# A new order for the 1284 listed jobs of a sketched-attention and mixture-of-experts kernel

## The chip, the core and the metric

The kernel runs on one core of one Trainium2 chip. The metric is the device time of one execution in microseconds. The engines are called by the profile's names: PE (matrix products; PEld loads their weights), DVE (VectorE), ACT (ScalarE), POOL (GpSimd) and SP, which here does nothing but issue DMAs. Each engine runs its instructions in the order in which the program lists them.

## The reference, cut to what matters

For 4 batches of 1088 rows, a polynomial attention is computed from sketches of q and k, and its output x (1088 by 128 per batch) goes into an attention with 4 experts, of which 2 are chosen per row.

```python
phi(x) = outer(S1 @ x, S2 @ x)                 # 8 x 8 = 64 features per head and row
kv, z  = phi(k).T @ v, phi(k).sum(rows)
x      = (phi(q) @ kv) / (phi(q) . z + 1e-6)   # 4 heads of 32 side by side: 128 columns
logits = x @ w_gate                            # the 2 largest of 4 experts, softmax weights w
a_e    = softmax(causal(scale * (x wq_e)(x wk_e).T))
out    = sum over the 2 chosen e of w_e * (a_e @ (x wv_e) @ wo_e)
```

## The kernel before

The kernel is a list of 1284 small jobs. Each `job(...)` has a name, one engine or a choice of two, its estimated length, what it reads and makes, and which buffers it holds. `Plan.run` (line 85) walks the text `ORDER` (line 21), a list of job numbers, and emits the jobs in that order. A letter behind a number says which of the two engines takes the job: for a copy `a` is ACT and `b` is DVE; for a product of features it depends on the job; for an idle matmul pair (`dummy`) `a` is PE and `b` leaves it out. A buffer from a pool goes to the next holder in the order of the list, so the list also decides who waits for which buffer. No engine reorders anything; a job that waits holds up all later jobs of its engine.

The work of one batch b has these stages, and the stages of neighbouring batches overlap.

- **Loads** of k, q and v (SP, for batch 0 also ACT). Batch 0's q comes in four loads, q0.0 and q0.2 on SP, q0.1 and q0.3 on ACT (line 436); k in two (line 430).
- **Batch 0's head** (`prepare`, `attend_rows`). DVE transposes k and q (`turn k0`, line 484; `turn q0`, line 494). PE projects them with the sketch (`project k0`, `k0+`, `q0`, `q0+`, line 562; the + parts hold the later columns). ACT or DVE copies half of each result (`low`), DVE adds the other half (`lift`, line 574), and DVE or POOL multiplies out the 64 features (`multiply`, line 580): two products for each of k0 and k0+, one for q0 and three for q0+. PE sums k features with v (`sums 0`, line 619), turns the q features (`turn qf`, line 666), multiplies by the sums (`numer 0`, line 692); DVE divides, PE turns x back.
- **Batches 1 to 3** (`prepare`, `attend_turned`): `sketch k`, `sketch q` (line 523), `back` (line 527), `features` (line 537), `sums` (line 627), `keep sums`, `repeat sums`, `fifth`, `keep rep`, `keep fifth`, `turn f` (line 805), `numer` (line 827), `turn rows` (line 839), stores of x and fetches of it in rows (line 857).
- **Choice of experts** (`choose_experts`): logits, comparisons, masks of bf16 that are stored to and fetched from memory (`fetch masks`, line 999; batch 0's first third is widened on PE instead, `widen`), `exponents`, `shares` (lines 945 to 957, POOL), `scale`.
- **Attention**: the 17 tiles of 64 rows of a batch come in groups 0 to 2 of 6, 6 and 5. `query b.n` (line 1066), `base`, `pick` (line 1079, needs the masks), `score b.i` (line 1104), `take` (line 1116, DVE), `exp` (ACT), `guard` (ACT or POOL), `invert`, `weigh` (line 1147, POOL), `turn A` (line 1152, DVE), then `sum b.n.j` (line 1180, PE, needs every `turn A` of its group), `keep V`, `patch V`, `spread V` (line 1207, POOL), `out` (lines 1251, 1277, 1301), `turn out`, `keep out`, `store out`.

PE has four pairs of PSUM banks for all of this. Group 0 of batch 3 is the last; its four expert products (`out 3.0.x`) end the kernel's matmuls, then three pieces are copied (`keep out 3.0.0` to `.2`) and stored.

Two small chains matter besides. The constant tables: `decode` (DVE) unpacks S1 and S2, `spread1` to `spread3` and `diagonal0` to `diagonal3` copy the tables into place on DVE, POOL and ACT, `rep16`, `repeat S2` (PE, line 362) and `keep S2` repeat one of them. And the gate: `load w4` fetches w_gate, `gate order` (POOL, line 294) reorders it, and all logits need it.

`dummy0` to `dummy39` are pairs of bf16 matmuls of 512 columns on a zeroed tile (line 250); their results are not used.

Of the kernel before, what the change touches and what calls it, by code (L numbers as in the profile page):

```python
# [24 lines left out]
61 414 403 130 134 419a 154 72 407 131 135 155 138 417a 75 73 408 412 136 74 23b 132 404 160 77 188 133a 161 137a 187  # L25
156 76 158 416a 162 163 166 157 141 192a 159 167a 164 190 191a 170 177 189 175 418a 165a 420 176 692 171 693 139 421
172 178 193 65 194 422b 411 423 140 209 210 195 182 196 66a 691 183 694 230 424 211 197 425 216 179 173 701 184 174a
428a 427a 143 180 202 231 181 702 426a 203 198a 232 199 212b 200 204 429 168 233a 153 217 254 253 185 201 213 205a 206
234 207 145 214 142 218 431 10b 430 208 258a 235 144 219a 257a 236 438 223 432 215 255 256 698 224 220 326 259 697 439
221 440 169a 327 329 225 260 148 330a 331a 226b 328 261 146 227 433 228 299 300 149 332 275 276 222 262 333 442a 283  # L30
301 441a 186a 284 229 263 277 268 434 264a 700 278 237 285 269 435a 238 436a 279a 270 437 271a 302 265 147 705 239 443
280 708 266 286 706 287a 281 272 282 240a 444 6b 32b 709a 243a 241a 303b 244 358 712a 273 304 245 305 274 151 359 446a
707a 445a 242a 267 711a 291 292 306 350 288 367 360 289 699 351 361 362a 366 293 294 369 290 343 246 26b 295a 368 713a
696 370 342 363 296 710a 344 14b 33b 345 297 247 464 465 371 364 298 447 715 714 352 466 695 467 469 703 307 372a 353
15b 354a 716a 717 346b 308 309 310 355 468 373 450 993 21b 474 718 721a 475 311 470 312 722a 719 316a 365 374 375 704
471 451 334 313b 347 335 314a 25b 720a 479 480 318 317 356 482 315b 336 723 481 348 320 484a 483a 448 357 43b 485 319
22b 337 321 323 338b 339 340 725 486 515 322 724 732 349 501 986 994 324a 516 517 547 548 341 494 449 487 502 503 495
488 733 508 476 509 472 726 990 510 546 734 545 727 376 377 477 736b 496 987 378 550a 150 379 489 992 549a 497a 380
504a 728 490b 511b 988 27b 518b 730a 498 519 152 735a 505 551 729b 522 381 478b 506 985 499 491 552 507 382 383 737
384 560 453 523 989 456 461 731 31b 385a 500 457 386b 592 512 513 492 389 591 520 39b 561 387b 388a 738 454 593 40b  # L40
41b 248 390 514 249 575 576 996 250 392 524 740b 525a 594 391 493 739a 526 251a 995 577 521 460 578 562 325 452 567
527 568 553 569 595a 563b 570 528 455 554 999 596 579a 7b 458 1002 580 473 555 758 619 13b 618 38b 759 1000 623a 529
760 571a 761 762 572 581 622b 624 530 556a 564 531 565 557 533a 620 597 532a 558 582 621 462 573 566 537 393 535a 534a
536 625 538 539 394 583 1001a 584 763 559 585 651 598 998 463 459 768 395 642 650 652 19b 20b 1004a 634 643 635 773
1005a 574 636 658 659 774 644 397 764 653 586 661 775 1003a 645 777a 660 776 1007b 1006a 646b 647 587a 778a 765 662
779 588 589 991 654b 627 648 769 663 780 637 664b 626 1009 590 1008 638b 599 600 628 649 655 1010b 1012 665 601 997
629 666 639 640 1011 602 603 741 1016a 630b 252 604 1015a 656 667 657 398 631 641 607a 606a 1013 770 541 605b 610 744
540 742 609 542 788 608b 789 816 543a 809 1014b 743 632 633 817 612 790 810 1017 1018 668 1019 811 1020 1021 745 669
781 795 818 670 671 672 782 783 796 812a 819b 1026 611 1027 791a 792 771 673 1028 1029a 674 772a 784b 793 797 785 675
1030a 676 1031 1022 677b 678b 681 842 1024a 679a 682 813 748 840 839 396 1023a 844a 841 802 747 680a 786 814 1025 803  # L50
804 615 614 843b 766 683 798b 613 820 794 845 815 805a 846 799 616b 1032 821 806 847 878 848 787 807 877 684 869 1034a
1033a 753 749 800 870 822 854 879 801 871 1052 913 808 912 862 855 861 849 856 885 1053 1054 886 914 746 767 1055 1056
872 916a 863 873a 850b 917a 751 851 918 852 915 874 617 823 864 824 887 825 875 888 919 865a 685 755 857a 750 853 921
37b 889a 866 880 42b 827a 826a 24b 858 1057 867 829a 868 876 1058 828b 544 920 890 831 830 859 686 860 689 922 923
881b 945 944 955 946 891 953 952 954 936 832 882 892 937 833 938 1139 754 947 30b 948b 924b 1138 44b 1141 1143a 956
1062 929 1140 883 1063 1060 884 1142a 925 836 957 1144 926 928 752 939 958a 1145 959 927 756 834 835 940a 1169 930
1168 941 931 1064 688 1170 837b 932a 1185 1184 960 961 838 1065 933 942 893 894 1186 949 950 943 895 951 896 934 1171
897 898 902a 935 901b 962 963 964 900b 1035 899a 1039 903 965 757 1172a 1146 1036 966 967 1187 1037 968 904 1147 969
970 1177 971a 1038 1153 972b 975 1176 906 974a 1042 976 905 973b 1212 1154 1043 1178 1155 1188a 1156a 1160 16b 17b
1179 978 1180a 1213 1061 1161 1211 1173 690 1214 907 908 1049 1157 909 1216a 1050 1148 1066a 1044 1189 9b 977 1190  # L60
1162 1059 1215a 1158 1191 1163 1164a 1217 1068 1067 1181 1149b 1174 1182 1218 1251 1071a 1252 687 1041 910a 1048 1040
1175 1183 1227 1254 1165 1150 1159 1228 1253 1255 1256 1046 1045 1166 1072b 1229 1244 1257b 1243 1230 1151 1245 1152
1073 1051 34b 1070 1069 1219 1167 1258 1220 1221 979 1074 1236 1231b 1232 1047 980 1259 1235 29b 1075 1246 1222 1247a
1223a 1192 1248 1237 1193 1224 1233 1249 1076 1234 1250 1194 1238 1110 1096 1239b 1260 1195 1225 36b 1226 1240 1097
1111 1089 1103 1241 1112 1242 1090 983 1196 1104 1197 1098 1099b 982 1105 1091 1261 1262 981 1113b 1198b 1201b 1199b
1114 1200a 1106b 1202 1263 1082 1264 1100 1265 1083 1204 1266 1077 1084 1107 1085b 35b 1101 1203 1267 984 1092b 1102
1115 1268 1205 1078b 1079 1108 1116 1086 1269 1093 1208 1087 1273b 1207 1094 1270b 1088 1274 1080 1095 8b 1272a 1206
# [1323 lines left out]
```

## Time and profile before

| | us |
|---|---|
| median of 3 runs (265.70 to 266.31) | 265.95 |
| profiled execution, its own time | 265.45 |
| its span, first to last instruction | 263.7 |
| PE busy | 256.1 (97%) |
| DVE busy | 208.5 (79%) |
| POOL busy | 161.0 (61%) |
| ACT busy | 104.3 (40%) |

The time of an execution holds the span and 1.75 us around it. Rows of the profile name an instruction by its line, engine and operation, and by the buffers that it writes and reads (`out<-in`), with shapes; `x` is a count. A bracket behind a row of the timeline is the idle time of the engine ahead of it and what ended it. Matmuls in 32-bit floats are two records each, and they are pipelined, so that records overlap. In tables by stretches the columns are busy time and count of PE, PEld, DVE, ACT and POOL, the granted clock, the share of DMA and GB/s.

### The profile page before, as it was taken

To read this page: it belongs to the slowest core of one execution; us is meant where nothing else is said; L and a number is where in the kernel's file an instruction comes from. 1 tells how busy PE (TensorE), PEld (TensorE's weight loads), DVE (VectorE), ACT (ScalarE), POOL (GpSimd) and SP (SyncE) were. 2 spreads that over 40 slices of the span, in tenths; PEclk is the share of its full clock that TensorE was granted. 3 is DMA by queue.
4 is the path that set the end of the run, shared out by engine and by line. 5 is a ranking of instruction groups with operands and counts; after the bars stand their busy time and mean duration, and the time that the engine had idled before them with its cause. 6 is when DMAs were issued, how large, how long until landed. Compare 5 with 4: busy or idle time off the path is not lost.

```text
span 263.7 us, 9228 instructions
## 1 busy us (share of the span) xinstructions
PE 256.1 (97%) x3807; PEld 193.4 (73%) x3807; DVE 208.5 (79%) x531; ACT 104.3 (40%) x278; POOL 161.0 (61%) x265
## 2 busy tenths in 40 slices
PE   7979999999999999999999999999999999999994
PEld 2967666755968877665797975665798875689984
DVE  5597999989998798999987288988885469895451
ACT  2333564665542315524613134635503164333020
POOL 6498478699677725198494894274734282533841
PEclk9999999999999999999999999999999999999999
DMA  7985769960288859806050390626114599210012
GB/s 149 187 144 144 145 144 177 175 134 1 46 169 162 124 149 213 149 14 149 2 88 4 83 167 30 163 51 152 14 32 81 103 221 194 50 44 2 5 32 56
DMA packets 87740, 27.35 MB, mean 104 GB/s; under 512 B 58577, under 2 KB 87057, under 8 KB 87697
## 3 DMA queue, kind: packets, MB, share of 16 engines
q1 hardware_dynamic: 85040, 26.08, 51.8%
q10 hardware_dynamic: 2656, 0.67, 1.1%
q8 instruction: 30, 0.49, 0.8%
q14 instruction: 14, 0.11, 0.2%
HBM read 22.22 MB, written 4.52 MB: 101 GB/s over the span
## 4 chain that ended last, share of the span: by engine, by line
PE 85%; DVE 9%; DMA 3%; issue 1%; ACT 0%; SPq 0%; ACTq 0%; DVEq 0%
PE pair L1180 28%; PE pair L1104 23%; PE pair L1066 10%; PE pair L1301 6%; PE pair L1251 3%; DMA mb<-md 3%; PE pair L523 3%; PE pair L627 3%; PE pair L827 2%; DVE fp L580 2%; PE pair L562 2%; DVE qs L1079 1%; DVE w L1116 1%; PE pair L1277 1%; DVE fp L805 1%
## 5 line engine op out<-in xcount | busy, mean ns | idle before, releaser
L1147 POOL TENSOR_SCALAR w<-w,rs,sh 128x448 f32<-128x448 f32 (+16 forms) x68 | 55.5, 822 | 39.8 <-DVE rs L1143 38.1
L1104 PE MATMUL pair<-xT,qs 128*128 128x384 f32 (+11 forms) x216 | 73.6, 477 | 0.3 <-DVE qs L1079 0.3
L1132 ACT ACTIVATE w<-w,mx 128x384 f32<-128x384 f32 (+16 forms) x68 | 52.4, 772 | 53.3 <-DVE mx L1116 45.9
L1116 DVE CUSTOM_DVE_ANT_0 w<-pair,mask 128x576 f32<-128x576 f32 (+13 forms) x68 | 48.5, 726 | 13.1 <-PE pair L1104 12.4
L1104 PEld LDWEIGHTS pair<-xT,qs 128*128 128x128 f32 x216 | 38.4, 190 | 24.9 <-issue 11.9
L1152 DVE STREAM_TRANSPOSE AT<-w 128x64 f32<-128x64 f32 (+16 forms) x68 | 50.8, 761 | 6.9 <-POOL w L1147 6.7
L1180 PE MATMUL pair<-AT,xra 32*128 32x160 f32 (+5 forms) x1136 | 44.9, 303 | 0.0
L1180 PEld LDWEIGHTS pair<-AT,xra 32*128 32x128 f32 x1136 | 41.7, 185 | 4.2 <-DVE mx L1116 1.8
L1207 POOL TENSOR_TENSOR agg<-agg,mb 128x768 f32<-128x768 f32 (+1 forms) x22 | 34.0, 1559 | 14.8 <-PE pair L1180 5.8
L1066 PE MATMUL pair<-xT,Mq 128*128 128x384 f32 (+1 forms) x96 | 33.7, 476 | 0.0
L193 ACT COPY agg<-pair 128x384 f32<-128x384 f32 (+1 forms) x27 | 11.8, 470 | 49.2 <-PE pair L1180 33.8
L1180 PEld LDWEIGHTS pair<-AT,xrb 32*128 32x128 f32 x752 | 26.3, 185 | 2.1 <-issue 2.0
L1180 PE MATMUL pair<-AT,xrb 32*128 32x160 f32 (+5 forms) x752 | 27.7, 289 | 0.0
L537 POOL TENSOR_TENSOR fp<-w 128x576 f32<-128x576 f32 x21 | 24.9, 1201 | 1.6 <-DVE w L527 1.1
L1066 PEld LDWEIGHTS pair<-xT,Mq 128*128 128x128 f32 x96 | 17.4, 190 | 10.9 <-issue 2.4
L1079 DVE COPY_PREDICATED qs<-mb,pair 128x768 f32<-128x768 uint16 (+1 forms) x24 | 23.1, 963 | 0.7 <-DMA mb<-md 0.3
L1301 PEld LDWEIGHTS pair<-Mo,agg 128*128 128x128 f32 x168 | 20.0, 192 | 2.2 <-issue 0.7
L1301 PE MATMUL pair<-Mo,agg 128*128 128x128 f32 x168 | 20.8, 277 | 0.0
L193 DVE COPY agg<-pair 128x384 f32<-128x384 f32 (+1 forms) x19 | 9.5, 519 | 9.7 <-PE pair L1180 9.7
L1140 POOL TENSOR_SCALAR rs<-zs 128x1 f32<-128x1 f32 x31 | 6.6, 213 | 17.1 <-ACT w L1132 12.9
L1143 DVE RECIPROCAL rs<-rs 128x1 f32<-128x1 f32 x68 | 9.1, 144 | 8.0 <-POOL rs L1140 6.6
L193 ACT COPY qs<-pair 128x384 f32<-128x384 f32 (+1 forms) x21 | 9.3, 455 | 10.9 <-PE pair L1066 10.9
(179 smaller groups left out, 311.7 us busy)
## 6 DMA issues: line engine op xcount, KB each, us to landing
xra<-xd SPq DMA_DIRECT2D x16, 192.0 KB, 5.5
xrb<-xd SPq DMA_DIRECT2D x16, 192.0 KB, 5.6
xrc<-xd SPq DMA_DIRECT2D x16, 160.0 KB, 5.1
mb<-md SPq DMA_DIRECT2D x4, 576.0 KB, 7.1
mb<-md SPq DMA_DIRECT2D x4, 480.0 KB, 6.9
mb<-md SPq DMA_DIRECT2D x6, 288.0 KB, 4.9
in<-in_k_dram SPq DMA_DIRECT2D x12, 136.0 KB, 3.1
in<-in_q_dram SPq DMA_DIRECT2D x3, 544.0 KB, 4.7
```

What stands on the lines that cost most here:

```text
L193: (nc.scalar.copy if eng == "ACT" else VEC[eng].tensor_copy)(o, i)
L537: VEC[e].tensor_tensor(out=f, in0=a[:, :, None, R : 2 * R].to_broadcast([128, j1 - j0, R, R]), in1=a[:, :, 0:R, None].to_broadcast([128, j ...
L1066: nc.tensor.matmul(plan[ps[x]][:, y, 0:w], Mq[:, ((1, 2), (0, 3))[x][y]], plan[xT][:, 64 * t0 : 64 * t1], start=True, stop=True)
L1079: nc.vector.copy_predicated(chosen(), rows(c), rows(plan[ps[x]]))
L1104: nc.tensor.matmul(plan[p][:, y, 0 : c1 - c0], plan[qs][:, 128 * t : 128 * t + 128], plan[xT][:, c0:c1], start=True, stop=True)
L1116: nc.vector.tensor_tensor_reduce(out=o, in0=src, in1=msk, scale=-1.0, scalar=mx[:, b, i, x - 1 : x] if x else 3e38, op0=ALU.add, op1=ALU.m ...
L1132: nc.scalar.activation(out=a, in_=a, func=ACTF.Exp, bias=mx[:, b, i, last : last + 1], scale=-1.0, accum_out=zs[:, b, i : i + 1])
L1147: nc.gpsimd.tensor_scalar(out=a, in0=a, scalar1=rs[:, b, i : i + 1], scalar2=plan[("sh", b)][:, i : i + 1], op0=ALU.mult, op1=ALU.mult)
L1152: nc.vector.transpose(dst[:, 0 : keys // 32, t], plan[A][:, 0:keys].rearrange("p (j s) -> p j s", s=32))
L1180: nc.tensor.matmul(plan[Vk[g // 2]][:, g % 2, lo : 32 * nt], plan[(f"xr{j // 12}", b)][rows, j % 12], a[rows, j, lo:], start=(j == 0), sto ...
L1207: nc.gpsimd.tensor_tensor(out=a, in0=a, in1=plan[mb][:, 2 * x : 2 * x + 2, 0:w], op=ALU.mult)
L1301: nc.tensor.matmul(plan[p][0:m, 0, 128 * x : 128 * x + 128], plan[agg][:, e, 128 * x : 128 * x + m], Mo[:, e], start=(e == 0), stop=(e == ...
```

## The change

Only the text `ORDER` differs: the same 1284 jobs in another order, with 87 of the choices of engine turned over. Line numbers stay as they are.

```diff
 ORDER = """
-0 1 2 3 4 78 79 46 12a 28a 5a 64 45 82 80 62 48 18a 55b 85 84 86 81 83 87 53b 56 11a 52b 54b 90 91 94 95a 96 98b 99 58
-92 93 104 100a 105a 88a 89b 101 108 68 97a 109a 400 399 103a 114 402 401 50 102b 49 110 106 115 113b 117a 57 59 107a
-111b 116b 124 51 125a 63 112a 406 118 70 120 60 409 410 119a 122 69 121a 47 126 123a 413 127 405 128 71a 415 67 129a
...
-1271a 1109 1276 1081 1117 1118 1119 1209a 1275 911 1277 1278 1210 1124a 1120b 1121 1122 1126 1125 1123a 1279 1128
-1127a 1281 1280 1129 1130 1282 1131 1136a 1137b 1283 1134b 1132a 1133b 1135a
+0 1 2 3 4 78 79 83 15a 80 45 21a 48 46 10a 81 90 53b 52b 91 54b 50 25b 18a 49 55b 5b 12a 14a 51 82 84 87 85 86 94 64
+63 95b 96 27a 57 56 58 92 99 93 98b 100a 65 104 97a 101 400 89b 66a 108 103a 88a 105a 114 68 69 106 102b 70 109a 401
+115 71a 110 116a 117a 107a 113a 402 399 118 124 111a 112a 59 60 120 61 406 119a 410 125a 122 405 121a 126 67 403 409
...
+1270a 1202 1115 1116 1081 1100 1205 1206 1101 1207 1208 1102 1274 1085b 1273a 1086 1275 1272b 1209a 1087 1088 1117
+1277 1118 17b 43b 6b 1276 1119 982 1124a 1120b 1121 1122 1210 1123a 1278 1126 1279 1128 40b 1129 23b 1125 29b 1281
+1283 1282 1127a 1130 1131 1280 1132b 1134b 37b 1133a 1136a 1135a 1137b
```

The head of the two lists, engine by engine:

```text
PE   before: 5 idle pairs | project k0 | project k0+ | project q0 | project q0+ | turn w0 | sums 0.0 | sums 0.1 | turn qf 0.3 | turn qf 0.0 | turn w2 | turn qf 0.1 | turn qf 0.2 | turn w1 | numer 0.0 | sketch k1
PE   after:  6 idle pairs | project k0 | 1 idle pair | project k0+ | repeat S2 | project q0 | project q0+ | sums 0.0 | turn w0 | turn w1 | turn w2 | sums 0.1 | turn qf 0.0 | turn qf 0.3 | turn qf 0.1 | turn qf 0.2 | numer 0.0 | sketch k1
DVE  before: decode | turn k0 | lift k0 | turn q0 | lift k0+ | multiply k0.0 | multiply k0+.1 | lift q0+ | lift q0 | multiply q0.0 | keep sums 0.0 | spread3 | multiply q0+.1 | turn k1
DVE  after:  decode | turn k0 | spread3 | low k0 | lift k0 | turn q0 | multiply k0.0 | lift k0+ | multiply k0+.1 | lift q0 | lift q0+ | multiply q0.0 | multiply q0+.2 | multiply q0+.0 | multiply q0+.1 | turn k1
POOL before: const | pick8 | ident | rep4 | diagonals | multiply k0.1 | spread v1 | multiply k0+.0 | spread1 | multiply q0+.2 | multiply q0+.0 | rep16 | mask | onehot | gate order | features k1
POOL after:  ident | const | diagonal2 | spread1 | diagonal3 | pick8 | rep16 | multiply k0.1 | spread v1 | multiply k0+.0 | gate order | onehot | rep4 | features k1
ACT  before: load q0.1 | load q0.3 | diagonals | low k0 | low k0+ | low q0 | spread v0 | low q0+ | spread2 | keep sums 0.1 | keep qf 0.3 ...
ACT  after:  load q0.3 | load q0.1 | diagonals | spread2 | low k0+ | keep S2 | spread v0 | low q0 | low q0+ | keep w | keep sums 0.0 | keep sums 0.1 | keep qf 0.0 ...
SP   before: load q0.2 | load q0.0 | loads of v | w0 | w2 | loads of k1 | w1 | w3 | v1.2 | w4
SP   after:  load q0.0 | load q0.2 | loads of v | w1 | w0 | w2 | loads of k1 | w3 | w4
```

Further on, the runs of `score`, `sum`, `query`, `sketch`, `numer` and `out` follow each other on PE in the same large order, with other neighbours inside the runs. `repeat S2` (65) stood on PE between `sums 1.1` and the first scores. `turn rows 3` (1035) now precedes the last `turn A` of batch 2, and `shares 3.0` (1064) comes right ahead of `weigh 2.13` (934) on POOL. `fetch masks 3.2` (1061) no longer follows two fetches of x on SP, and `spread V 2.1.1` (906), whose buffer it takes over, comes behind `scale 3.0` (1066) and `weigh 3.9` (1174) on POOL. At the end `turn out 3.2` (1279) precedes `mix V 3.0.1` (1125) on DVE, `keep out 3.0.0` goes from ACT to DVE, and its store from ACT to SP.

Of the 87 turned choices, 8 are idle pairs (7 are run where 5 were), 29 are `guard` (15 from ACT to POOL, 14 back), 37 are `keep` copies (17 from ACT to DVE, 20 back), and the rest single copies, products, one `scale` and one store.

More of the change, by code (lines that the diff above doesn't have):

```diff
@@ L27 @@
[L27 to L46, printed above, removed]
@@ new lines @@
+1147 1066a 1174 906 1148 1149b 1156a 907 1150 1212 1211 1157 971a 909 1175 972a 1189 974a 976 1037 1158 1061 1151 975
+1038 1160 1216b 1161 973b 1214 1215a 1190 978 1046 1217 1213 1051 1191 1040 1176 1177 1218 1178 1152 1044 1162 977
+1179 908 1049 1228 1159 1227 1180a 1219 1220 1251 1163 1181 1059 910a 1182 1229 1164b 1254 1165 1252 1042 1221 1253
+911 1166 1230 1068 1067 1072a 1244 1070 1231a 1071a 1069 690 1183 1255 1243 1167 1236 1232 1073 1256 1074 1235 1257a
+1222 1245 1075 979 1223b 1224 1258 1041 1233 1237 36b 1246 1225 1043 1047 980 1259 1234 1076 1260 1192 1247a 1238 1048
```

60 lines of the change are left out of this document (37 added, 23 removed).

## The prediction

> **What bounds the kernel now.** I read the busy shares first, then the chain that ended last, then busy time by stretches.
>
> ```profile
> PE 256.1 (97%) x3807; PEld 193.4 (73%) x3807; DVE 208.5 (79%) x531; ACT 104.3 (40%) x278; POOL 161.0 (61%) x265
> PE 85%; DVE 9%; DMA 3%; issue 1%; ACT 0%; SPq 0%; ACTq 0%; DVEq 0%
> ...
> 36.00:56.00 20.00, 19.75 (x297) 12.81 (x296) 19.44 (x53) 11.67 (x38) 15.28 (x28) 1.00 1.08 170
> 76.00:208.00 132.00, 132.00 (x2066) 100.59 (x2064) 107.04 (x259) 49.17 (x132) 78.34 (x121) 1.00 0.49 96
> 208.00:220.00 12.00, 11.75 (x58) 8.21 (x57) 9.30 (x23) 6.20 (x18) 7.96 (x12) 1.00 1.03 198
> ```
>
> The fourth row's first busy figure is PE: 132.00 of 132.00. The two other stretches lose 0.25 us each. So from some 20 us on PE sets the end, and a new order of the same matmuls can win only where PE waits or does useless work: in the head and in the tail. In 36 to 56 DVE is as full (19.44 of 20.00), which matters below.
>
> The head, by the order of time on PE:
>
> ```profile
> 1.31 4.45 PE L250 MATMUL pair<-idle 128*128 128x512 bf16 x10 [1.31 <-DVE idle L243]
> 6.33 6.33 PE L562 MATMUL pair<-SD,in 128*128 128x128 f32 x36 [0.57 <-DVE in L484]
> ...
> 20.66 1.60 PE L523 MATMUL pair<-in,SK 32*32 32x288 f32 x64
> ...
> 6.30:8.40 2.10, 2.07 (x10) 2.10 (x11) 1.00 1.24 253
> 8.40:10.50 2.10, 2.10 (x11) 2.10 (x11) 1.00 1.25 200
> 10.50:12.50 2.00, 2.00 (x19) 1.97 (x17) 1.00 0.76 120
> ```
>
> Ten idle matmuls, a hole of 0.57 us, then the projections (L562); the last three rows are those alone. They come 10 or 11 in 2.1 us before 10.5 and 19 in 2.0 us after it: PE runs at half pace up to there. From L523 (sketch k1, 20.66) on, PE is full. I measure the head by when sketch k1 can start. What holds it is a chain on DVE:
>
> ```profile
> 4.78 1.41 DVE L484 STREAM_TRANSPOSE in<-in 128x576 f32<-128x576 f32 x2
> 8.82 0.42 DVE L574 TENSOR_TENSOR w<-pair,w 128x256 f32<-128x256 f32 x1 [2.64 <-ACT w L193]
> 9.16 1.36 DVE L494 STREAM_TRANSPOSE in<-in 128x384 f32<-128x384 f32 x2
> 11.01 0.49 DVE L574 TENSOR_TENSOR w<-pair,w 128x320 f32<-128x320 f32 x1 [0.48 <-ACT w L193]
> 11.41 3.12 DVE L580 TENSOR_TENSOR fp<-w 128x512 f32<-128x512 f32 x2
> 14.46 0.81 DVE L574 TENSOR_TENSOR w<-pair,w 128x384 f32<-128x384 f32 x2
> 15.30 1.73 DVE L580 TENSOR_TENSOR fp<-w 128x768 f32<-128x768 f32 x1
> ...
> 17.19 0.81 DVE L193 COPY SK<-SK 32x48 f32<-32x48 f32 x1
> 18.03 0.85 DVE L580 TENSOR_TENSOR fp<-w 128x512 f32<-128x512 f32 x1
> 18.81 1.36 DVE L488 STREAM_TRANSPOSE in<-in 128x512 f32<-128x512 f32 x2
> ```
>
> DVE waits 2.64 us for project k0 and its copy, 0.48 for project k0+, and is then busy until the last feature (18.88) and turn k1 (20.17), which lets sketch k1 go.
>
> **The change, part by part. Idle matmuls.** Six pairs now run ahead of project k0, one more than before: 12 at 0.43 (4.45 for 10) from 1.31 end near 6.5, against a start at 6.33. The extra pair is hidden to 0.2 us by turn k0, which runs to 6.19. The seventh, ahead of project k0+, costs 0.43 to 0.86 there; its cover is turn q0 and multiply k0.0 on DVE, which now come before lift k0+; without that cover the whole chain is late by as much. What the filled hole does to the pace no row shows. Bounds: fast from the start of project k0, or from 10.5 as now. Project k0 (8 records) then takes 0.85 to 1.7 us and ends between 7.4 and 8.3; I take 7.8, in the middle, and keep both.
>
> The Trainium skill ("TensorE: Matmul & The Clock Gate", Part 1) says that the array's rate doubles after a busy window of about 3.4 us, and that the windows run free of the kernel's start. By it a filled hole brings the rise one window forward or changes nothing, as the phase falls; the doubling in the rows agrees.
>
> **Features on VectorE.** Low k0 moves from ACT to DVE (an ACT copy in either place: about 0.4), spread3 (0.81 of the chain now, at 17.19) goes into DVE's idle time before it, two multiplies of q0 move from POOL to DVE. Prices:
>
> ```profile
> 15.15 2.81 POOL L580 TENSOR_TENSOR fp<-w 128x512 f32<-128x512 f32 x2 [0.53 <-DVE w L574]
> ...
> L537 DVE TENSOR_TENSOR fp<-w x3: 695/753/793, 87.1 to 124.9; 128x576 f32<-128x576 f32 x3
> ...
> 11.57 1.17 ACT L193 COPY vp<-w 64x1152 f32<-64x1152 f32 x1
> 12.70 0.48 ACT L193 COPY w<-pair 128x384 f32<-128x384 f32 x1
> 2.10 1.07 ACTq L436 DMA_DIRECT2D in<-in_q_dram  x2
> ...
> in<-in_q_dram ACTq DMA_DIRECT2D x2, 136.0 KB, 5.2
> ...
> 10.54 2.57 SPq L436 DMA_DIRECT2D in<-in_k_dram  x4
> wgr<-in_moe_w_gate_dram SPq DMA_DIRECT2D x1, 2.0 KB, 3.1
> ```
>
> The same product costs DVE 0.695 for 576 elements in its cheapest record (1.21 ns each) and 1.73 for 768 (2.25 ns) while POOL multiplies beside it from 15.15. The four q multiplies are 2304 elements: 2.8 us without POOL, 5.2 beside it. In the new list POOL's next job after its two k products is the copy of w_gate (gate order), and that load is issued behind the four loads of k1. These begin when project k0+ is done and take 2.57 to issue; the load of w_gate takes 3.1 to land. With project k0+ done near 9.5, that is past 15; POOL then stands still for much of the q features. I take 3.2.
>
> DVE, worked forward: low k0 from 7.9 (0.4), lift k0 0.42, turn q0 1.36: to 10.1. The q loads are shared out in another order over the same two queues, all four are needed, and the last of ACT's row lands 5.2 after an issue near 2.6, so by 7.8: cost nothing, and 0.9 us of cover (turn q0 begins at 8.7). On SP the load of w1 goes ahead of the k1 loads; the queue stands still before 10.54 anyway. Multiply k0.0 (512) 0.6 to 1.15, say 0.8, to 10.9; lift k0+ 0.49; multiply k0+.1 1.8 (768 elements, POOL beside it) to 13.2. Low q0 and low q0+ on ACT follow the copy of v, which stays at 11.57 if v lands as now: 1.17, about 0.3 (low q0 has half the columns of the 0.48 row) and 0.48, to 13.5, so the second lift ends near 14.0. Features 3.2 to 17.2, against 18.88: 1.7 earlier. Turn k1 follows to 18.6 (the k1 loads, issued a little earlier, have landed by then), and PE reaches sketch k1 over its last turn of q features and numer 0.0 by the same 1.7 earlier. The ends: features 2.8 and a fast pace, 2.5 gained; features 5.2 and a slow pace, 0.8 lost.
>
> The skill ("SBUF — State Buffer", Who interferes with whom) says that a VectorE instruction with two SBUF inputs and a GpSimd one that reads SBUF lock each other out for a whole instruction. 1.73 against 0.93 for 768 agrees. By it POOL's later casts, if w_gate lands early, hold up one feature each; then the sum is 266.4, as the second rival has it.
>
> **The stretch after sketch k1.** Repeat S2 moves from here into the head, where PE waits anyway:
>
> ```profile
> 33.29 0.63 PE L362 MATMUL pair<-ident,rep 32*128 32x32 f32 x4
> 33.85 1.46 PE L1104 MATMUL pair<-xT,qs 128*128 128x192 f32 x6
> ```
>
> Start to start it held PE for 0.56: gained. Counting runs of one kind of matmul after sketch k1, the new list has 73 where the old has 70. A change of kind has no row of its own; between nothing and 0.28 each (half of the 0.56, which holds two changes and the work), I take 0.13: 0.4 lost. The macro order of PE (which score, sum, sketch and query runs follow each other) is the same, so its load is. DVE takes the small copies keep rep 1.0 and keep fifth 1 and gives keep sums 1; none has more columns than the copy of 0.29 in the tail's rows, so up to 0.3 is lost in the full stretch, and I count 0.3. The 87 jobs that change engine are mostly guards (15 one way, 14 back) and V copies (17 against 20): level.
>
> The one wait there that the chain shows:
>
> ```profile
> 208.78 6.91 DMA mb<-md
> ```
>
> The masks of batch 3 landed at 215.7 and cost PE 0.25 of 208 to 220. In the new list their fetch no longer stands behind two fetches of x on SP, but spread V 2.1.1, which frees its buffer, stands behind two more jobs on POOL: level. Waits of a new list at new places can't be read here; the old one has 0.5 us in two stretches. I allow 0.5 more, with 0 and 3 as ends.
>
> **The tail.**
>
> ```profile
> 259.80 0.29 DVE L193 COPY ob<-pair 128x128 f32<-128x128 f32 x1 [1.94 <-PE pair L1277]
> 260.78 0.27 ACT L193 COPY ob<-pair 128x128 f32<-128x128 f32 x1 [0.45 <-ACT ob L193]
> 261.07 0.37 ACTq L1283 DMA_DIRECT2D out_dram<-ob  x1
> ```
>
> The last store waits on ACT behind another copy and store. Its copy moves to DVE (259.80 and 260.1) and its store to SP, so the last issue starts near 260.5: 0.5 gained. Turn out 3.2 goes ahead of mix V 3.0.1 on DVE, which out 3.0.1 needs two matmul groups later: 0 to 0.1.
>
> **Sum** on the profiled execution (span 263.7, time 265.45): -1.7 - 0.56 + 0.4 + 0.3 + 0.5 - 0.5 = -1.56, or 263.9. The median of the runs shown is 265.95, 0.5 higher than the profiled execution, so the forecast on that scale is 264.4; the unknowns of the head alone put it between 263.5 and 265.3.
>
> **Rivals.** *The pace rises no sooner* (the filled hole does nothing): project k0 ends at 8.3, the chain is 0.5 later: 264.9. For it: no row shows what raises the pace. It lies inside the forecast's own range.
>
> *Features beside POOL, or DVE's full stretch.* If w_gate lands early, the features cost 5.2 and end at 19.2, 0.3 late; or the gain meets DVE at 97% in 36 to 56 and is gone by numer 1. For it: that stretch. Against: POOL's queue. Then +0.3 or 0 stands in place of -1.7: 266.1 to 266.4; I take 266.1.
>
> *Slower: the last transposes of batch 2.*
>
> ```profile
> 194.87 2.24 DVE L1152 STREAM_TRANSPOSE AT<-w 128x1024 f32<-128x1024 f32 x2 [0.26 <-POOL w L1147]
> 199.28 1.30 DVE L839 STREAM_TRANSPOSE w<-xT 128x1088 f32<-128x1088 f32 x1
> ...
> 186.00 0.24 POOL L945 TENSOR_TENSOR ch<-ch,c 128x18 f32<-128x18 f32 x1
> 187.80 0.20 POOL L953 TENSOR_TENSOR ch<-ch 128x9 f32<-128x9 f32 x1
> ...
> 197.72 0.38 PE L1180 MATMUL pair<-AT,xra 32*128 32x160 f32 x1
> ```
>
> Sum 2.2.0 (197.72) needs the last turn A of its group, done at 197.11: 0.6 of slack. The new list puts shares 3.0 (186.00 to 188.00 now) right ahead of weigh 2.13 on POOL, which that turn waits for, and turn rows 3 (1.30, now after it) ahead of the turn on DVE. If nothing of it is hidden, the sums start 1.3 + 2.0 - 0.6 = 2.7 late: 267.1. Against it: shares 3.0 waits for nothing of this group and can be done early. It decides from 1.6 us on (no gain left) and makes the kernel slower by more than 0.2% from 2.1. Sums of other groups stand the same way.
>
> **Chances.** Forecast with its own range, slow pace included, 0.50; features beside POOL or the full stretch 0.22 (0.15 the same, 0.07 slower); late sums 0.16, all slower; a list better than read (POOL still, no waits of its own: 263.0) 0.12. A measurement of this kernel can tell about 0.2% (0.5 us) from no change. So faster 0.62, same 0.15, slower 0.23. The range 262.8 to 267.1 leaves out the worse part of the late sums and little below.
>
> **What would show it.** Last feature of q0 near 17.2 and sketch k1 near 19 (the head); DVE's q products near 1.2 ns an element with POOL idle; no L362 at 33; last store issue 0.5 us closer to PE's end; PE full from there on. Wrong, if PE shows waits over 1 us after 30 us, or if sketch k1 starts after 20.

## The result, and the profile after

| | before | after |
|---|---|---|
| median of 13 runs each | 265.86 (263.87 to 266.31) | 263.08 (262.28 to 263.86) |
| profiled execution, its own time | 265.45 | 263.49 |
| its span | 263.7 | 261.8 |

The ratio of the runs is 0.9911, with a 95% interval of 0.9888 to 0.9934: faster, by 2.4 us (1.8 to 3.0); the medians differ by 2.8. The forecast was 264.4, in a range of 262.8 to 267.1.

I read the profile after in the order of the prediction: busy shares and chain, the stretches, the head, the tail. First the page:

```profile
PE 254.9 (97%) x3811; PEld 192.2 (73%) x3811; DVE 208.4 (80%) x529; ACT 105.6 (40%) x279; POOL 157.5 (60%) x266
...
PE 84%; DMA 8%; DVE 5%; POOL 1%; issue 1%; SPq 0%; ACT 0%; DVEq 0%; POOLq 0%; ACTq 0%
```

The second row is the chain that ended last: PE has 84% of it for 85 before, DMA 8% for 3, DVE 5% for 9.

Then the table by stretches (busy time and count of PE, PEld, DVE, ACT, POOL):

```profile
20.00:36.00 16.00, 15.56 (x260) 10.97 (x262) 14.91 (x57) 7.52 (x25) 10.66 (x27) 1.00 0.68 147
36.00:56.00 20.00, 19.67 (x292) 11.92 (x263) 19.28 (x50) 10.87 (x30) 16.53 (x30) 1.00 1.08 176
76.00:208.00 132.00, 132.00 (x2064) 100.99 (x2045) 107.69 (x261) 51.89 (x141) 80.72 (x131) 1.00 0.44 92
208.00:220.00 12.00, 12.00 (x57) 8.64 (x56) 9.34 (x19) 5.00 (x12) 5.93 (x7) 1.00 0.93 185
```

PE is full from 76 to 220, the wait of 0.25 us for the masks of batch 3 is gone, and 36 to 56 loses 0.33 where it lost 0.25. The first stretch loses 0.44. Before, it lost 0.12:

```profile
20.00:36.00 16.00, 15.88 (x300) 11.56 (x296) 13.52 (x53) 7.58 (x22) 10.31 (x25) 1.00 0.62 132
```

Behind sketch k1 the timeline of PE shows two waits in all, one ahead of the first scores and one ahead of numer 1:

```profile
32.28 1.89 PE L1104 MATMUL pair<-xT,qs 128*128 128x64 f32 x8 [0.38 <-DVE qs L1079]
...
52.37 2.18 PE L827 MATMUL pair<-fp,kvr 32*32 32x288 f32 x64 [0.33 <-DVE w L527]
```

No sum waits, so the rival that ended slower did not come about.

The head on PE, then on DVE and POOL, from the timeline:

```profile
1.31 4.66 PE L250 MATMUL pair<-idle 128*128 128x512 bf16 x12 [1.31 <-DVE idle L243]
6.67 1.13 PE L562 MATMUL pair<-SD,in 128*128 128x128 f32 x8 [0.70 <-DVE in L484]
...
12.97 1.12 PE L619 MATMUL pair<-vp,fp 128*64 128x33 f32 x32 [0.86 <-POOL vp L193]
14.03 0.87 PE L390 MATMUL pair<-ident,AT 128*128 128x128 f32 x6
14.83 1.36 PE L619 MATMUL pair<-vp,fp 128*64 128x33 f32 x40
16.12 2.18 PE L666 MATMUL pair<-ident,fp 128*128 128x128 f32 x18
18.23 0.92 PE L692 MATMUL pair<-kvz,fp 128*64 128x66 f32 x24
19.09 1.60 PE L523 MATMUL pair<-in,SK 32*32 32x288 f32 x64
```

```profile
11.05 0.96 DVE L580 TENSOR_TENSOR fp<-w 128x768 f32<-128x768 f32 x1
...
13.13 3.55 DVE L580 TENSOR_TENSOR fp<-w 128x768 f32<-128x768 f32 x4
16.60 1.36 DVE L488 STREAM_TRANSPOSE in<-in 128x576 f32<-128x576 f32 x2
19.27 0.17 DVE L699 TENSOR_SCALAR den<-pair 128x12 f32<-128x12 f32 x1 [1.31 <-PE pair L692]
```

```profile
11.09 1.83 POOL L193 COPY vp<-w 64x1024 f32<-64x1024 f32 x1 [1.22 <-DMA w<-in_v_dram]
...
17.59 0.18 POOL L294 COPY wg<-wgr 128x2 f32<-128x2 f32 x1 [3.52 <-DMA wgr<-in_moe_w_gate_dram]
```

Sketch k1 starts at 19.09 where it started at 20.66. But look at who waits. DVE ends turn k1 at 17.96 and then waits 1.31 us for PE. PE has been without a break since 12.97, when it got v from POOL: 0.86 us of waiting stand there. DVE's chain, which held the head before, is no longer last; the copy of v and then PE itself are. The copy had itself waited 1.22 us for the load of v, and the chain that ended last begins with loads, of q and then of v, which lands at 10.94:

```profile
1.87 4.53 DMA in<-in_q_dram
6.42 4.52 DMA w<-in_v_dram
```

The tail, with DVE's two copies in one row and two stores on SP:

```profile
258.37 0.49 DVE L193 COPY ob<-pair 128x128 f32<-128x128 f32 x2 [1.49 <-PE pair L1277]
258.64 0.27 ACT L193 COPY ob<-pair 128x128 f32<-128x128 f32 x1 [4.51 <-PE pair L1277]
258.69 0.83 SPq L1283 DMA_DIRECT2D out_dram<-ob  x2
258.94 0.38 ACTq L1283 DMA_DIRECT2D out_dram<-ob  x1
```

The gain of the profiled pair in three parts, by the start of sketch k1 and the end of PE's last record (259.98 before, 258.56 after): head 1.57; from sketch k1 to PE's end 239.32 before and 239.47 after, so 0.15 lost; from there to the end of the span 3.75 before and 3.22 after, 0.53 gained. Together 1.95, which is the difference of the spans. The second pair of profiles (before_again and after_again below) splits otherwise: 1.81 in the head, 0.33 lost behind it, 0.11 gained in the tail, together 1.60.

### The profile page after: what moved, and what is told of

The parts are those of the page before. It is cut to its first block, busy times and chain, and to the rows that moved or that the text cites. A ratio compares the mean times of both kernels' runs of the same rounds, so it can differ in the third digit from the quotient of the medians.

```text
span 261.8 us, 9228 instructions
## 1 busy us (share of the span) xinstructions
PE 254.9 (97%) x3811; PEld 192.2 (73%) x3811; DVE 208.4 (80%) x529; ACT 105.6 (40%) x279; POOL 157.5 (60%) x266
## 4 chain that ended last, share of the span: by engine, by line
PE 84%; DMA 8%; DVE 5%; POOL 1%; issue 1%; SPq 0%; ACT 0%; DVEq 0%; POOLq 0%; ACTq 0%
PE pair L1180 28%; PE pair L1104 24%; PE pair L1066 9%; PE pair L1301 7%; DMA mb<-md 4%; PE pair L1251 3%; PE pair L523 2%; PE pair L827 2%; DMA in<-in_q_dram 2%; DMA w<-in_v_dram 2%; PE pair L627 2%; DVE w L1116 1%; PE pair L1277 1%; DVE fp L805 1%; PE pair L619 1%; PE pair L692 1%
## 5 line engine op out<-in xcount | busy, mean ns | idle before, releaser
L1147 POOL TENSOR_SCALAR w<-w,rs,sh 128x256 f32<-128x256 f32 (+14 forms) x68 | 56.8, 840 | 34.4 <-DVE rs L1143 32.8
L1104 PE MATMUL pair<-xT,qs 128*128 128x320 f32 (+9 forms) x216 | 74.0, 478 | 0.4 <-DVE qs L1079 0.4
L1132 ACT ACTIVATE w<-w,mx 128x64 f32<-128x64 f32 (+15 forms) x68 | 52.4, 772 | 45.8 <-DVE mx L1116 40.6
L1116 DVE CUSTOM_DVE_ANT_0 w<-pair,mask 128x64 f32<-128x64 f32 (+14 forms) x68 | 48.3, 723 | 15.4 <-PE pair L1104 13.0
L1104 PEld LDWEIGHTS pair<-xT,qs 128*128 128x128 f32 x216 | 38.8, 190 | 25.9 <-issue 11.1
L1152 DVE STREAM_TRANSPOSE AT<-w 128x320 f32<-128x320 f32 (+15 forms) x68 | 51.2, 762 | 3.4 <-POOL w L1147 3.0
L193 ACT COPY agg<-pair 128x384 f32<-128x384 f32 (+1 forms) x31 | 13.2, 463 | 45.5 <-PE pair L1180 44.0
L537 POOL TENSOR_TENSOR fp<-w 128x576 f32<-128x576 f32 x19 | 22.6, 1209 | 1.6 <-DVE w L527 1.1
L1301 PEld LDWEIGHTS pair<-Mo,agg 128*128 128x128 f32 x168 | 20.6, 192 | 2.4 <-issue 0.5
L1203 DVE COPY_PREDICATED agg<-mb,pair 128x384 f32<-128x384 uint16 (+1 forms) x24 | 12.7, 557 | 4.8 <-ACT agg L193 4.4
L1132 ACT ACTIVATION_READ_ACCUMULATOR w<-w,mx 128x1 f32 x68 | 12.8, 189 | 0.0
```

The lines of the kernel that those rows point to most:

```text
L193: (nc.scalar.copy if eng == "ACT" else VEC[eng].tensor_copy)(o, i)
L537: VEC[e].tensor_tensor(out=f, in0=a[:, :, None, R : 2 * R].to_broadcast([128, j1 - j0, R, R]), in1=a[:, :, 0:R, None].to_broadcast([128, j ...
L1104: nc.tensor.matmul(plan[p][:, y, 0 : c1 - c0], plan[qs][:, 128 * t : 128 * t + 128], plan[xT][:, c0:c1], start=True, stop=True)
L1116: nc.vector.tensor_tensor_reduce(out=o, in0=src, in1=msk, scale=-1.0, scalar=mx[:, b, i, x - 1 : x] if x else 3e38, op0=ALU.add, op1=ALU.m ...
L1132: nc.scalar.activation(out=a, in_=a, func=ACTF.Exp, bias=mx[:, b, i, last : last + 1], scale=-1.0, accum_out=zs[:, b, i : i + 1])
L1147: nc.gpsimd.tensor_scalar(out=a, in0=a, scalar1=rs[:, b, i : i + 1], scalar2=plan[("sh", b)][:, i : i + 1], op0=ALU.mult, op1=ALU.mult)
```

## Theories and experiments

The step from one record of PE to the next says at which pace PE runs. In the profile before it falls from 0.21 to 0.11 us at 10.6 us, in the profile after from 0.43 to 0.22 (idle matmuls, whose records are twice as long) at 5.2. Four theories came up in turn:

1. **Pace.** The rise comes late in most executions of the kernel before, because of the hole ahead of project k0; the idle pairs bring the gain.
2. **Features**, as forecast: what DVE multiplies brings it, and DVE, full in 36 to 56, is what can take it away.
3. **Transfers.** A lead of the head is lost near 53 us, where the DMA engines are full and PE waits for its own program.
4. **A start at 11 us.** Two instructions on DVE and POOL start almost together, and which is first decides 0.8 us.

Each run stands beside runs of the kernel before on the same chip; their medians are given, since they move from one set of runs to the next (265.11 here and 265.80 in the last set, both on one chip). The first four shared 265.11.

**pairs_alone**

```diff
-11a 52b 54b 90 91 94 95a 96 98b 99
+11a 14a 52b 54b 90 91 94 95a 96 27a 98b 99
```

(The words 14b and 27b, which leave the pairs out, go from further down.)

> The kernel before, with only the idle pairs of the new list: a sixth pair ahead of project k0 and one between project k0 and project k0+. Theory 1 (pace): in the kernel before the step from one idle matmul or projection record to the next halves at 10.6 us, in the kernel after at 5.2 us; the hole before project k0 is what delays it, in most executions, and the times of the kernel before lie in two groups (263.9 to 264.2 in 3 of 13, 265.6 to 266.3 in 10 of 13) because it doesn't in all. Then the pairs alone bring nearly all runs to the low group: a median of 264.0, with the step halved before 8.6 us in the profile. Theory 2 (features, as forecast): what counts is what DVE multiplies; the pairs are worth 0 to 0.5 us: a median of 265.4 to 265.9, with both groups still there.

264.70 (264.11 to 265.69); ratio 0.9983 (0.9963 to 1.0003), between the two expectations. 9 of 12 runs lie from 264.1 to 265.0 and 3 above 265.6, where 15 of 35 runs of the kernel before lie under 264.85 and 20 from 265.1 up. The pace rose at 4.8 us, sketch k1 started at 19.79. So fewer runs lie in the upper group, as theory 1 has it, but with 3 of 12 beside 20 of 35, and an interval that holds 1, little is shown; the pairs don't bring 2 us.

**five_pairs**

```diff
-14a
+14b
-27a
+27b
```

> The kernel after, with five idle pairs ahead of project k0 and none behind it, as before. Theory 1 (pace): most runs lose the early rise: a median near 264.5 to 265, with a run or two left at 262.5 to 263, and a profile whose step halves near 10.6 unless it fell on a lucky run. Theory 2 (features): 263.1 to 263.6, the pairs being worth 0 to 0.5 us.

263.10 (262.49 to 266.16); ratio 0.9939 (0.9913 to 0.9966): the number of theory 2. Its profile says that this is no plain "the pairs are worth nothing":

```profile
51.03 2.11 PE L827 MATMUL pair<-fp,kvr 32*32 32x288 f32 x56 [0.23 <-DVE w L527]
53.85 0.68 PE L827 MATMUL pair<-fp,kvr 32*32 32x288 f32 x8 [0.71 <-issue]
54.45 8.11 PE L1104 MATMUL pair<-xT,qs 128*128 128x512 f32 x22
```

Sketch k1 started at 17.98 and numer 1 at 51.03, 1.3 earlier than in the profile after (52.37), yet the scores behind it (L1104) start at 54.45 as they do there (54.48). Numer 1 is cut in two after 56 of its 64 records, and what ends the wait is no semaphore ("issue"). The part on DMA queues for 48.4 to 53.9 us shows what else went on:

```profile
q1 hardware_dynamic: 2905, 1.06, 94.7%
q8 instruction: 1, 0.02, 1.6%
```

The share is that of sixteen engines: 94.7% full with data, and one packet of 16 KB of kind "instruction". There are 30 such packets in the whole span, one for every 254 records of PE and PEld together. When that one was moved, and how long numer 1 took up to the scores:

```text
profile       numer 1   packet moved    to the scores   break: after record, until
five_pairs     51.03    51.1 to 52.5        3.42        56, 53.85
tail_back      51.60    51.2 to 52.5        2.82        52, 53.80
q_on_pool      51.78    51.1 to 52.4        2.73        52, 53.90
after_again    51.60    49.0 to 50.4        2.11        none
after          52.37    49.9 to 51.2        2.11        none
```

The breaks end 1.3 to 1.5 us behind the packet, and they fall on the same count of PE's records (727 matmuls and as many weight loads, 1454, ahead of each): the two kernels with seven pairs have four more matmuls ahead, and break four records earlier in numer 1. So PE waits for a block of its program. The Trainium skill ("Runtime: NRT & Kernel Launch", Instruction fetch mechanics) says that programs come in blocks of 16 KiB, 256 instructions, and that crossing into the next is mostly hidden; the size agrees, and it was not hidden here.

The full DMA engines alone don't tell why the packet was late: the profile after has the same 94.7% from 48.4 to 53.9 us, its packet was moved 1.3 us earlier, and PE did not break.

**q_on_pool**

```diff
-113a
+113b
-111a
+111b
```

> The kernel after, with the products q0+.2 and q0+.0 on POOL as before. Theory 1 (pace): PE's head is set by pace and by the turns and copies, POOL stands idle there anyway: 263.1 to 263.7. Theory 2 (features): the last feature of q0 comes 1.0 to 1.7 us later, sketch k1 starts near 20.3, and the time is 264.1 to 264.6.

263.51 (262.99 to 265.08, and one run of 267.22 with a granted clock of 0.994); ratio 0.9938 (0.9916 to 0.9960). PE's rows:

```profile
16.95 1.09 PE L666 MATMUL pair<-ident,fp 128*128 128x128 f32 x8 [0.49 <-POOL fp L580]
...
18.83 1.60 PE L523 MATMUL pair<-in,SK 32*32 32x288 f32 x64
```

PE waits 0.49 us for POOL's products. Sketch k1 at 18.83 stands against 18.29 in after_again below, whose copy of v took as long: 0.54. From the end of that copy to sketch k1 it is 6.88 us, against 6.16 to 6.26 in the profiles with the products on DVE and an early pace: 0.6 to 0.7. That is what the two products on VectorE are worth in these profiles. Theory 2 expected sketch k1 near 20.3 and a time of 264.1 at least; the time that came is the one theory 1 gave.

**head_alone**: the words of the kernel after up to 413 (sketch k1), then what is left of the words of the kernel before.

> The list of the kernel after up to sketch k1, then the jobs that are left in the order of the kernel before (its tail included). Both theories put the gain into the head and 0.5 us into the tail: 263.5. If, beside this, the new neighbours in 36 to 56 us cost the 0.4 us by which the lead shrinks there (sketch k1 1.57 early, numer 1 only 1.15 early), 263.1; if the lead shrinks there just as much with the old neighbours, DVE at 19.4 of 20.0 being what takes it, 263.5 or above.

264.10 (263.62 to 265.54); ratio 0.9959 (0.9937 to 0.9981): 0.6 above the 263.5 that was expected. Two idle pairs of the old list fell behind sketch k1 and cost PE 0.85 us there; without them it would, by estimate, be near 263.25, between the 263.1 and the 263.5 of the expectations. Sketch k1 (18.86) to PE's end is 240.15, which is the 239.32 of the kernel before and 0.83. So the new neighbours behind the head cost next to nothing in sum, and what it lacks against after besides stands in the tail of the old list (4.06 us from PE's end to the span's, 3.22 in after).

The next four shared a chip with 265.64 for the kernel before.

**late_loads** and **late_loads_pairs** (the first from five_pairs, the second from the kernel after): load q2 (695) goes behind fetch x 0.10, turn q2.1 (704) behind store x 1.2, and load k3.2 and k3.0 (987, 985) behind store masks 1.

```diff
-705 695 280
+705 280
...
-290 704 359
+290 359
...
-711a 987 246
+711a 246
...
+146 695 354b
...
-467 985 469
+467 469
...
+450 704 309
...
+470 987 985 312
```

> The kernel five_pairs, with the load of q2 (544 KB, issued at 46.6 us there) put behind the last fetch of x of batch 0, turn q2.1 (0.74 us on DVE, at 54.1 us there) 10 us later, and two of the four loads of k3 (272 KB) behind the stores of the masks of batch 1. Theory 3 (transfers): in five_pairs the lead of the head (sketch k1 at 17.98, numer 1 at 51.03) is lost inside numer 1, where PE waits 1.3 us in all for a block of its own program, whose packet of 16 KB is moved from 51.1 to 52.5 us, late, because the DMA engines are full from 36 to 56 us. With less to move the packet comes before 51, numer 1 runs without the break, and the scores behind it start 0.7 to 1.3 us earlier than 54.45: 262.0 to 262.5. Theory 2 (DVE full from 36 to 64 us): the packet matters little, the gain is what DVE is rid of, 0.3 to 0.7 us, and the same with seven pairs: 262.4 to 262.8.

> The same moves of the loads of q2 and k3 and of turn q2.1 in the kernel after, with its seven idle pairs. There numer 1 (52.37 to 54.48) has no break, its packet is moved from 49.9 to 51.2, and what leads to numer 1 is the fetch of the masks of batch 0 (33.1 to 42.6), issued ahead of q2. Theory 3 (transfers): little to win, 262.7 to 263.1. Theory 2 (DVE full): 0.3 to 0.7 us, 262.4 to 262.8, as with five pairs.

late_loads 262.28 (261.90 to 263.29), ratio 0.9877 (0.9841 to 0.9912); late_loads_pairs 262.51 (262.15 to 262.90), ratio 0.9881 (0.9847 to 0.9915). In late_loads the packet was moved from 50.2 to 51.4, and numer 1 runs whole:

```profile
51.39 2.27 PE L827 MATMUL pair<-fp,kvr 32*32 32x288 f32 x64 [0.24 <-DVE w L527]
53.59 8.11 PE L1104 MATMUL pair<-xT,qs 128*128 128x512 f32 x22
```

The scores start 0.86 us earlier than in five_pairs, as theory 3 expected. But that the moved loads brought the packet forward is not shown. The packet starts anywhere from 49.0 to 51.2 in after_again, after and tail_back, whose programs are the same up to there. And from 45 to 51.2 us the DMA engines were no emptier: 117.0% busy with data in late_loads (0.95 MB), 98.6% in five_pairs (1.19 MB). The second kernel gave 0.36 against after_again on this chip, which is theory 2's number; it may be chance, since the intervals overlap.

**after_again** and **before_again**: the two kernels unchanged.

> The kernel after, unchanged, as the base of the others and for a second profile: 262.9 to 263.3. If the pace depends on where the execution falls, the step between PE's records halves at another moment than 5.2 us, between 4.7 and 8.6.

> The kernel before, unchanged, for a second profile. Theory 1 (pace), for the two groups of times alone: if the profiled execution takes under 264.9 us, the step between PE's records halves before 7 us; if it takes over 265.1, it halves near 10. If the groups have another cause, pace and time don't go together.

after_again: 262.87 (262.30 to 263.46), ratio 0.9893 (0.9854 to 0.9932). Its pace rose near 5.9, but what makes its profile better is elsewhere, in the rows of DVE, POOL and PE:

```profile
11.14 1.71 DVE L580 TENSOR_TENSOR fp<-w 128x768 f32<-128x768 f32 x1
```

```profile
10.98 1.05 POOL L193 COPY vp<-w 64x1024 f32<-64x1024 f32 x1 [0.98 <-DMA w<-in_v_dram]
```

```profile
12.17 1.12 PE L619 MATMUL pair<-vp,fp 128*64 128x33 f32 x32
...
18.29 1.60 PE L523 MATMUL pair<-in,SK 32*32 32x288 f32 x64
```

The same program, 0.80 us earlier at the first sum and at sketch k1. Here POOL's copy of v starts ahead of DVE's product; in the first profile the product starts 0.04 ahead of it. Whoever is second pays: copy 1.05 and product 1.71, or copy 1.83 and product 0.96. The rule of the Trainium skill that the prediction cites ("SBUF — State Buffer", Who interferes with whom: a VectorE product and a GpSimd instruction lock each other out) agrees in both directions; the prediction had only one of them.

before_again: 264.78 (263.89 to 265.86), ratio 0.9974 (0.9944 to 1.0005), though it is the kernel before itself; so much do two sets of runs of one program differ. The profiled execution took 264.77, and its pace had risen by the start of project k0 at 6.89, as theory 1 expected for a time under 264.9:

```profile
1.31 4.18 PE L250 MATMUL pair<-idle 128*128 128x512 bf16 x10 [1.31 <-DVE idle L243]
6.89 2.25 PE L562 MATMUL pair<-SD,in 128*128 128x128 f32 x18 [1.40 <-DVE in L484]
```

18 records in 2.25 us, where the first profile of this kernel had 36 in 6.33. Sketch k1 starts at 20.10 instead of 20.66.

The next three shared 265.36.

**extra_pe** (idle matmuls added, their results overwritten)

```diff
         def repeat_sums():
+            for _ in range(4 if b == 1 else 0): nc.tensor.matmul(plan[rep[0]][:, 0], idle[:, 0:128], idle, start=True, stop=True)
```

> The kernel after, with four idle matmuls of 512 columns (0.85 us on PE at full pace) put into repeat sums 1, near 35 us, between sketch k1 and numer 1. As the prediction counted repeat S2 (PE sets the end from sketch k1 on): all of it shows, logits 1 starts 44.3 us behind sketch k1 instead of 43.45, and the time is 263.7 to 263.9. If DVE and the transfers set the pace between sketch k1 and numer 1: logits 1 stays 43.3 to 43.6 behind sketch k1, and the time at 262.9 to 263.2.

263.74 (262.94 to 264.94); ratio 0.9947 (0.9920 to 0.9974).

```profile
62.94 0.69 PE L878 MATMUL pair<-xT,wg 128*32 128x288 f32 x8
```

Logits 1 (L878) starts 44.11 behind sketch k1 (18.83), against 43.43 in the profile after: 0.68 of the 0.85 shows (by PE's end 0.94: 240.41 from sketch k1 against 239.47). The two waits shown above are shorter here, 0.51 for 0.71 together. So PE sets the pace there but for those waits, as the prediction counted repeat S2, and theories 2 and 3 fall as an account of that stretch; theory 3 keeps the break in numer 1.

**copies_on_act** (from late_loads)

```diff
-427b
+427a
-426b
+426a
```

> The kernel late_loads, with the small copies keep rep 1.0 and keep fifth 1 (0.28 and 0.15 us on DVE) on ACT as in the kernel before. If DVE sets the pace between sketch k1 and numer 1: numer 1 comes 32.6 to 32.8 us behind sketch k1 instead of 33.06, and the time is 261.9 to 262.1. If the transfers do (masks of batch 0): DVE waits longer for them instead, 33.0 stays, and the time is 262.2 to 262.4.

263.69 (262.60 to 263.98); ratio 0.9918 (0.9888 to 0.9948). Numer 1 comes 33.27 behind sketch k1, not earlier than the 33.06 of late_loads: PE now waits 0.24 us for ACT's copy ahead of sketch q1. Taking the two copies off DVE gained nothing. Its profile has the product first at 11 us (copy 1.85), and sketch k1 at 18.82 where late_loads had 18.33, so its time doesn't compare with that kernel's.

**tail_back**

```diff
-1280 1132b 1134b 37b 1133a 1136a 1135a 1137b
+1280 1134b 37b 1136a 1135a 1137b 1132a 1133b
```

> The kernel after, with the end of the list as before: keep out 3.0.0 on ACT behind keep out 3.0.2, and its store on ACT. As predicted, the last store is issued 0.5 us later against PE's end, the span ends 3.7 to 4.1 us behind PE instead of 3.2 to 3.6, and the time is 263.4 to 263.6. Rival (the end is set by how long the stores take to land, SP's included): no change, 262.9 to 263.1.

263.69 (262.93 to 265.03); ratio 0.9932 (0.9903 to 0.9962). The last store is issued at 259.99, on ACT behind copy and store, and the span ends 3.74 us behind PE instead of 3.22:

```profile
259.69 0.27 ACT L193 COPY ob<-pair 128x128 f32<-128x128 f32 x1 [0.45 <-ACT ob L193]
259.99 0.37 ACTq L1283 DMA_DIRECT2D out_dram<-ob  x1
```

The old tail took 3.74 to 4.06 us behind PE in all its five profiles. The new one took 3.22 or 3.23 in seven of nine, 3.41 in copy_first and 3.64 in after_again, so the half microsecond is not gained in each execution.

**copy_first** (from late_loads, beside 265.80 for the kernel before; the memsets write a column that is no longer used)

```diff
-            m = 4 * (c1 - c0)
+            m, _ = 4 * (c1 - c0), [nc.vector.memset(warm, 0.0) for _ in range(5 if (e, nm, c0) == ("DVE", "k", 6) else 0)]
```

> The kernel late_loads, with five memsets of one column on DVE (0.06 us each in their cheapest record, near 0.3 in all) ahead of multiply k0+.1. In the profiles the copy of v on POOL (spread v1) and multiply k0+.1 on DVE start within 0.2 us of each other near 11 us, and the one that starts second takes long: the copy 1.05 us and the product 1.64 to 1.79 where the copy is first (five profiles), the copy 1.82 to 1.85 and the product 0.96 where the product is first (five profiles, after among them); two profiles of the one kernel after differ in this, and in sketch k1 by 0.8 us (19.09 and 18.29). Theory 4 (that start decides 0.8 us of each execution): with the product put 0.3 us later the copy is always first, 1.05 us in the profile, sketch k1 at 18.0 to 18.5, and the times lose their upper part: 261.8 to 262.4, one in six above 262.8 at most. Rival (the spread of the times has another source, the break in numer 1 or the transfers): the profile shows the copy first, but times still reach from 261.9 to 263.5, half of them above 262.6.

263.04 (262.06 to 264.04); ratio 0.9896 (0.9868 to 0.9925). A miss on the times, and a useful one; PE's rows, then POOL's:

```profile
6.29 4.07 PE L562 MATMUL pair<-SD,in 128*128 128x128 f32 x18 [0.53 <-DVE in L484]
...
13.05 1.13 PE L619 MATMUL pair<-vp,fp 128*64 128x33 f32 x32
```

```profile
10.99 1.06 POOL L193 COPY vp<-w 64x1024 f32<-64x1024 f32 x1 [0.59 <-DMA w<-in_v_dram]
```

The copy is first, 1.06. But with five pairs this execution fell on the late pace: project k0 and k0+ take 4.07 us for 18 records (2.25 in before_again), the step falls near 10.2, and the first sum starts at 13.05, a microsecond behind the copy. Its times stand in two groups, 262.06, 262.28, 262.56 and 263.53 (the profiled one), 263.83, 264.04. That spread is what the rival expected. That the late pace makes the upper group is argued from the one profiled execution.

Over all profiles: with five pairs the pace was late in 2 of 6 (before, copy_first), with seven in 0 of 8. Among the kernels with the new head, all but this one let chance decide at 11 us: product first in 5, copy first in 5.

One figure on record bears on theory 1 and is in none of the profiles. The mean granted clock of a run is 0.994 or less in 28 of the 88 runs of the kernel before that stand beside the experiments. These take 265.36 us at least (median 266.0; the other 60 have 264.9). Of the 105 runs of the kernels with the new head, five pairs or seven, it is so in one, the 267.22 of q_on_pool. At the 0.50 that the clock column shows at the end of the profile before (263.50 to 263.75), 0.994 would be some 3 us at half clock in all (an estimate). No such execution was profiled, so where they lie is not known. The late pace alone it cannot be: the profile before has that at a mean of 0.999. So part of the gain in the medians may be that the new head seldom meets this: without these runs the medians of the four sets of the kernel before are 0.3 to 0.8 us lower.

## Why the prediction was right, and where it was not

**What bounds the kernel: right.** PE from sketch k1 on; extra_pe shows it, and what after leads by at logits 1 (62.52 against 63.75) is still there at PE's end.

**Idle pairs: in the bounds, wrong about where.** Project k0 ended near 7.6 to 7.8, the value taken. The hole was not filled: turn k0 waited for k and ended at 6.5, and 0.70 us of hole stayed. The pace was fast from the start of project k0, the better end of the bounds. That is no gain by itself in every execution: the old list reaches it in part of its executions with a hole of 1.40. What the pairs may do is keep it from being late (0 of 8 profiles against 2 of 6, too few to be sure). A late pace cost 0.6 (20.66 against 20.10) to 0.8 us (19.17 in copy_first, 18.33 in late_loads) at sketch k1; five_pairs, without the added pairs, has the median of the kernel after (263.10 and 263.08). The free-running windows of the Trainium skill, as the prediction told them, fit: one program rises early or late.

**Features on VectorE: the number right, the reason wrong.** This is the step that failed. The prediction let sketch k1 follow from the last feature (17.2) and turn k1 (18.6), and got "near 19"; measured 19.09. But the features ended at 16.68 and turn k1 at 17.96, better than forecast, and sketch k1 waited for PE, whose work began only when POOL had copied v. What would be late next, once DVE waited less, was taken to be DVE's own chain still; next were the load of v, POOL's copy of it and 6.12 us of PE work behind that. The other profiles bear it out: in nine of the eleven with the new head sketch k1 starts 6.16 to 6.26 us behind the end of that copy; the other two are q_on_pool (6.88) and copy_first with its late pace (7.12). That 19.09 meets "near 19" is luck: the same program starts sketch k1 at 18.29 in after_again. The q products took 3.55 us for the 3.2 counted, and 2.90 in after_again. The 1.8 us for multiply k0+.1 "beside POOL" cost DVE only 0.96 in that profile, since it came first, and POOL paid. POOL stood idle beside the q features (3.52 us of waiting for w_gate), as forecast. Undone, the move of the two products costs 0.5 to 0.7, not the 1.7 of the head.

**Stretch after sketch k1: signs right, the sum 0.5 over.** Counted +0.64 (S2 -0.56, changes of matmul kind +0.4, copies +0.3, waits +0.5), measured +0.15. S2 holds by extra_pe; the copies cost nothing that copies_on_act could take back. The other terms I read from the repeated profile after_again, job by job from start to start: up to numer 1, changed neighbours of 0.05 to 0.2 each make a net +0.6, and waits +0.47 (0.34 at score 0.7, for masks, and 0.13 ahead of numer 1; in the first profile the wait of 0.38 stands at the first scores instead). Then come the waits of the old list that are gone, which the prediction called level: 0.25 for the masks of batch 3 and 0.08 in numer 1. -0.56 + 0.6 + 0.47 - 0.33 is +0.2, between the 0.15 and the 0.33 of the two pairs of profiles.

**Tail: right** in most executions, 0.53 for 0.5, and undone by tail_back.

**Rivals.** The pace that rises no sooner is real, but it is a matter of the execution, and was seen only with five pairs. Late sums: not seen. "Better than read, 263.0" is where the median came out, though its condition, no waits of the new list's own, did not hold. The median is 1.3 under the forecast: 0.4 is the difference of the sums (1.95 for 1.56), and 0.9 is the scale, for the forecast set the median 0.5 above the profiled execution, and the kernel after has it 0.4 below. Why is not shown; that its profiled execution has the product first at 11 us fits.

One sum of the prediction doesn't come out. Its ends for the head, 2.5 gained and 0.8 lost in place of 1.7, give 263.6 and 266.9 on the scale of the medians, not 263.5 to 265.3; neither the forecast nor its range rests on it.

**What stays open.** What of the head's gain besides the features (0.5 to 0.7) and the pace belongs to spread3, low k0, the shared loads and the order on DVE was not tried singly. Nor was an earlier load of v, which the rows of the head ask for. Why a packet of program is moved late in one execution and early in another is open, and so is where the runs with a granted clock of 0.994 lose their time. Whether late_loads (262.28) and late_loads_pairs (262.51) beat the kernel after (262.87 beside them) is likely from the medians, but the intervals against before overlap; the second has the narrowest times of all, 262.15 to 262.90.

## What to carry to other kernels

When a chain in the head is shortened, list every input of the engine that comes next, with its time of arrival; the next one late here was a load and its copy that nobody had touched. Take two profiles of one program before believing a difference under 1 us: here three things (pace, who starts first, a block of program) each moved an execution by 0.6 to 1.3 us. A sum that charges a new list for waits should also credit the waits of the old list that go: here 0.47 came and 0.33 went.

## What the runs showed of the hardware

- The granted clock reads 1.00 in the head of the profile before, while a projection's record takes 0.21 us up to 10.6 and 0.11 after it: the step between records shows what the clock column doesn't.
- PE can stand still for its own program: 16 KB packets, one per 254 records, and breaks in numer 1 until 1.3 to 1.5 us after a late one, with 94.7% of the DMA engines' time in data. The same 94.7% in the profile after went with an earlier packet and no break.
- DVE's product of two SBUF inputs and POOL's copy hold each other up (product 0.96 and copy 1.82 to 1.85, or copy 1.05 and product 1.64 to 1.79), and the order of their starts, 0.02 to 0.2 us apart, decides who pays 0.7 to 0.8 us.
- The mean granted clock of a whole run is 0.994 or less in 28 of 88 runs of one list and in 1 of 105 runs of the lists with the new head; the 28 are 1.1 us slower than the other 60 by their medians.
